# Turns of pairs 16 to 18 issued together, with the loads of two batches held behind them

## Chip, cores and metric

One Trainium2 chip, one core. The metric is device time in microseconds of one execution, lower is better; runs are compared by their median.

## The reference

Attention with 16 extra "beacon" keys ahead of the 576 causal ones, for 8 batches of 8 heads of 64, and behind it a mixer with a low-rank token mix and a two-layer MLP over the 512 channels:

```
scores = (q @ concat(beacon_k, k).T) / sqrt(64), causal over the last 576 keys
attn   = softmax(scores) @ concat(beacon_v, v)
x      = attn as (8, 576, 512)
u      = x + (x.T @ U @ V).T
out    = u + relu(u @ w_ch1) @ w_ch2          # 512 -> 2048 -> 512
```

## The kernel before

The work is in f16, with f32 in PSUM. A pair is two heads of one batch; there are 32 pairs, four to a batch, so pairs 16 to 19 are batch 4 and pairs 20 to 23 batch 5. The tokens of all batches are cut into blocks of 512 for the MLP, whose work is cut into small units (four matmuls each) that wait in a list.

The order of everything is written out by hand: a string `SCRIPT` of short words, which `step` turns into instructions one after the other. Each engine works through its own instructions in that order and waits where an operand isn't there. A plain number n takes n MLP units from the list. The other words that matter here:

- `k5`, `q5`, `b5`, `v4`: loads of that batch's k, q, beacon k and v, issued on POOL (GpSimd) with a cast from f32 to f16 (`k_loads`, `q_loads`, L184 and L190; `v_loads`, L187 and L197). k and q go to the tiles `hd` (the first tokens) and `st` (the other 512); there are two of each, so batch n + 2 takes the place of batch n.
- `GkA16`: regroup, the copy of pair 16's k from `st` into the pair's tile `pr` (three of them). The letter before the number names the engine: A for ScalarE (ACT, L518), V for VectorE (DVE, L247), G for POOL.
- `R16`: the turn of pair 16, a DMA transpose of `pr` into a tile `raw` (three of them), issued on SP (L277). A batch's first turned pair issues ahead of it two more DMA transposes that turn the first tokens of all its heads (L270, `qT<-hd`, `kT<-hd`).
- `TkV16`, `TqA16`: the copy of the turned k or q from `raw` into the order of tokens, on the engine of the letter (DVE L285, ACT L518).
- `Sa16`, `Sb16`: the pair's scores (PE, L311) and their exponentials (ACT, L317). `M16`: the causal mask (DVE, L298 and L300). `A16.0`: exp times v for one head (PE, L335), then its sums' reciprocal and the product (DVE, L343 and L344).
- `X3.0` to `X3.2`: the low-rank mix of a batch; `x12`: a DMA transpose of attention output (SP, L355).
- MLP units: first layer (PE, L435), ReLU on ACT (L439) or DVE (L441); second layer (PE, L452), the sum with `ut` on DVE (L465), the store on SP (L470). The first unit of a block also issues four DMA transposes of `uT` into `ut` on SP (L425).
- `Z16`: a copy of one element of pair 16's `raw` into a scratch element, on POOL. `step` has the word; the string before doesn't use it.

Eight PSUM banks are shared by all of PE's outputs, so PE stops when ACT and DVE don't empty them. The kernel's guard (a check of the softmax sums at the end, with a general path that isn't taken) plays no part here.

Of the kernel before, what the change touches and what calls it, by code (L numbers as in the profile page):

```python
# [27 lines left out]
def kernel(  # L28
# [605 lines left out]
    def step(t):  # L634
# [58 lines left out]
        TqV8 2 GkV10 1 A6.0 GqA10 TqA10 q3 1 A7.1 A7.0 2 X1.0 X1.1 X1.2 TkA10 TqV9 TkV9 1 TkA8 1 Sa9 Sa8 3 Sb8  # L693
        1 k3 GqA11 1 v3 Sb9 M8 2 A8.1 A8.0 1 GkV12 1 GqV12 Sa10 1 M9 GkV11 R12 Sb10 1 M10 1 TkV11 1 A10.0
        TqA11 4 GkA13 A9.1 A9.0 Sa11 1 TkV12 GqV15 Sb11 1 k4 A10.1 2 GkA14 GqV13 1 TqA12 b5 Sa12 1 GqA14 M11
        R13 R14 3 GkA15 Sb12 1 A11.0 1 TkV13 M12 A11.1 q4 b4 TqA13 Sa13 R15 A12.0 TkA14 TqV14 1 TqV15 1 GkA16
        GqA16 1 R16 2 Sb13 v4 1 A12.1 M13 X2.0 2 Sb14 GkA17 A13.0 X2.1 TkV15 X2.2 A13.1 Sa14 GqA17 R17 Sb15 k5
        q5 GqA18 1 M14 1 Sa15 x12 3 TkV16 A14.1 TqA16 1 A14.0 k6 4 M15 GkA18 x13 1 R18 TkA17 1 TqV17 Sb16 2
        Sa16 A15.1 GkA19 M16 2 A15.0 TqA18 2 GqA19 x14 GkV20 x15 1 GkA21 1 R19 Sa17 1 A16.0 Sb17 2 GqV20 A16.1
        1 M17 TkA18 Sb18 X3.0 2 X3.1 1 Sa18 A17.0 1 GqA21 M18 1 X3.2 1 TkA19 R20 1 R21 1 GkV22 b6 1 TqA19  # L700
        A18.0 A18.1 v5 1 A17.1 Sa19 4 x18 1 Sb19 TqV20 TkV20 2 M19 GqA22 1 x16 R22 Sb20 A19.1 q6 Sa20 3 M20 1
        TkA21 x17 1 A19.0 1 TqA21 1 A20.0 TqV22 v6 1 GkV23 GqA23 1 x19 R23 Sa21 TkV22 X4.0 1 k7 1 Sb21 1 M21 1
        X4.1 1 A20.1 Sa22 1 A21.0 1 GkV25 GqV24 1 TqA23 GkV24 1 b7 R24 1 TkV23 Sb22 1 q7 A21.1 x20 X4.2 1
        GqA26 M22 GqV25 4 Sa23 x21 A22.0 TkA24 1 Sb23 R25 1 M23 2 A22.1 1 TqA24 A23.1 GkA26 1 R26 Sa24 2 A23.0
        2 Sb24 x22 2 TkA25 TqA25 v7 5 GqV27 1 M24 GkV27 Sa25 2 x23 TkV26 1 A24.0 R27 1 Sb25 TqV26 M25 X5.0
        A24.1 GqV28 2 Sb26 1 GkA28 R28 A25.0 2 x24 Sa26 TqV27 1 X5.1 4 X5.2 1 GkV30 1 TkA27 M26 1 TkV28 A25.1
        GkV29 Sa27 GqV29 2 Sb27 1 A26.0 x25 1 R29 1 M27 A26.1 TqV28 GqA30 1 R30 A27.1 GkV31 2 Sa28 A27.0 1 x26
        1 TqV29 Sb28 2 M28 2 GqV31 TqA30 1 TkA29 TkA30 Sa29 1 X6.0 R31 Sb29 A28.1 x27 A28.0 4 TkV31 2 TqV31 1
        M29 1 Sa30 1 A29.0 2 x28 X6.1 2 Sb30 A29.1 X6.2 4 x29 Sa31 M30 10 Sb31 A30.0 A30.1 2 x30 M31 4 A31.0
        A31.1 2 X7.0 4 x31 1 X7.1 3 X7.2 2  # L710
    """

    with tc.manual_schedule(engines={ENG.PE, ENG.Activation, ENG.DVE, ENG.SP, ENG.Pool}):
# [118 lines left out]
```

## Time and profile before

| | |
|---|---|
| median of 3 runs | 359.29 us (359.05 to 359.36) |
| the profiled execution's own time | 361.73 us |
| its span, first to last instruction | 360.1 us |
| granted TensorE clock, mean | 0.993 |
| PE busy | 347.2 us, 96% |
| ACT, DVE, POOL busy | 205.2, 189.9, 84.0 us |
| DMA queue of POOL's loads | 17.54 MB written, 51.8% of 16 engines' span |
| DMA queue of SP's transfers | 25.14 MB, 34.9% |

PE is the matmuls, PEld the weight loads that run beside them; SPq and POOLq are the sequencers that issue DMAs. An idle time in square brackets is that of the engine just before the instruction, with what ended it. All starts are in us from the span's start.

### The profile page before, as it was taken

The numbers are of one execution on the slowest core, as the hardware profiler recorded it, in microseconds if no ns is written. First come the engines' busy times: TensorE is split into PE (matmuls) and PEld (weight loads), VectorE is DVE, ScalarE is ACT, GpSimd is POOL, SyncE is SP. The second block draws the span as 40 slices with busy tenths as digits, with TensorE's granted clock in tenths as the row PEclk, the third lists the DMA queues.
The fourth block names the chain that finished last, engine by engine and source line by source line (L and its number), as shares of the span: only waits on it lengthen the run. The fifth ranks groups of instructions, "written<-read, shape, count | busy, mean of one in ns | idle before, by whom it ended". The sixth has DMA issues, their size and how long they took to land.

```text
span 360.1 us, 7694 instructions
## 1 busy us (share of the span) xinstructions
PE 347.2 (96%) x3022; PEld 177.2 (49%) x3022; DVE 189.9 (53%) x530; ACT 205.2 (57%) x432; POOL 84.0 (23%) x123
## 2 busy tenths in 40 slices
PE   7789999999999989999999999999999999999995
PEld 3455478844545435454444444454544544444444
DVE  3775355546649454574767427675554447313311
ACT  4885867399579868658653963678335302401300
POOL 7966648601308005400630050000000000000000
PEclk9989999999999999999999999999999999999998
DMA  9999999992959999996899694563333123013112
GB/s 191 174 172 187 183 191 164 202 160 40 164 127 129 117 162 111 175 223 106 94 163 194 139 107 107 111 116 61 88 100 66 20 76 103 16 58 90 31 48 76
DMA packets 134396, 43.57 MB, mean 121 GB/s; under 512 B 106545, under 2 KB 130353, under 8 KB 134353
## 3 DMA queue, kind: packets, MB, share of 16 engines
q0 software_dynamic: 69008, 17.54, 51.8%
q1 hardware_dynamic: 64752, 25.14, 34.9%
q8 instruction: 25, 0.41, 0.5%
q10 hardware_dynamic: 592, 0.34, 0.3%
q14 instruction: 19, 0.15, 0.1%
HBM read 37.63 MB, written 9.44 MB: 131 GB/s over the span
## 4 chain that ended last, share of the span: by engine, by line
PE 86%; DMA 6%; DVE 2%; ACT 2%; SPq 1%; issue 1%
PE cps L452 35%; PE gps L435 32%; PE po L335 8%; PE sps L311 7%; DMA raw<-pr 4%; DMA sth<-in_q_dram 2%; ACT expt L317 1%; DMA stm<-in_q_dram 1%; PE tps L257 1%; PE ups L394 1%; PE ups L401 1%; PE qtp L375 1%; SPq L190 1%; DVE xb L344 1%; SPq L184 1%
## 5 line engine op out<-in xcount | busy, mean ns | idle before, releaser
L317 ACT ACTIVATE expt<-sps 128x496 f16<-128x496 f32 (+2 forms) x256 | 111.6, 544 | 43.2 <-PE sps L311 39.2
L452 PE MATMUL cps<-w,gT 128*128 128x512 f16 (+1 forms) x656 | 134.2, 353 | 0.0
L435 PE MATMUL gps<-uT,w 128*128 128x512 f16 x576 | 132.7, 379 | 1.1 <-DVE xb L344 1.1
L439 ACT ACTIVATE gT<-gps 128x512 f16<-128x512 f32 x86 | 52.2, 625 | 70.4 <-PE gps L435 70.2
L452 PEld LDWEIGHTS <-gT 128*128 128x128 f16 x656 | 60.5, 98 | 57.5 <-issue 4.4
L435 PEld LDWEIGHTS <-w 128*128 128x128 f16 x576 | 53.0, 98 | 65.1 <-issue 3.5
L441 DVE TENSOR_SCALAR gT<-gps 128x512 f16<-128x512 f32 x58 | 40.0, 690 | 49.5 <-PE gps L435 48.6
L465 DVE TENSOR_TENSOR ob<-cps,ut 128x512 f32<-128x512 f32 (+1 forms) x33 | 22.2, 674 | 47.0 <-PE cps L452 46.6
L335 PEld LDWEIGHTS <-expt 128*128 128x128 f16 (+1 forms) x960 | 36.0, 99 | 14.5 <-DVE expt L298 4.0
L197 POOL DMA_DIRECT2D vs<-in_v_dram x50 | 40.0, 811 | 7.2 <-DMA st<-in_k_dram 4.0
L335 PE MATMUL po<-vs,expt 128*128 128x65 f16 (+1 forms) x960 | 39.2, 195 | 2.3 <-ACT expt L317 1.4
L311 PE MATMUL sps<-qT,kT 64*128 64x80 f16 (+4 forms) x384 | 35.7, 282 | 2.1 <-ACT expt L317 1.2
L344 DVE TENSOR_TENSOR xb<-po,rec 128x320 f16<-128x320 f32 x64 | 31.5, 492 | 2.2
L298 DVE TENSOR_TENSOR expt<-expt,bigmask 128x512 f16<-128x512 f16 x64 | 26.7, 418 | 9.2 <-ACT expt L317 9.2
L343 DVE RECIPROCAL rec<-po 128x5 f32<-128x5 f32 x64 | 12.0, 188 | 28.0 <-PE po L335 27.2
L311 PEld LDWEIGHTS <-kT 64*128 64x128 f16 x384 | 12.5, 94 | 24.4 <-issue 16.4
L187 POOL DMA_DIRECT2D vs<-in_beacon_v_dram x10 | 5.4, 540 | 68.1 <-PE po L335 68.0
L408 DVE TENSOR_TENSOR uT<-ups,xt 128x240 f16<-128x240 f32 (+3 forms) x40 | 15.6, 450 | 7.2 <-PE ups L401 7.2
L518 ACT ACTIVATE pr<-st 128x512 f16<-128x512 f16 x26 | 16.8, 658 | 0.8 <-DMA st<-in_k_dram 0.8
L190 POOL DMA_DIRECT2D st<-in_k_dram x8 | 6.8, 856 | 40.7 <-ACT gT L439 22.9
L518 ACT ACTIVATE qT<-raw 128x512 f16<-128x512 f16 x10 | 11.1, 1105 | 5.3 <-DMA raw<-pr 5.3
L300 DVE TENSOR_TENSOR expt<-expt,mask 80x80 f16<-80x80 f16 x64 | 12.2, 191 | 0.0
(78 smaller groups left out, 170.7 us busy)
## 6 DMA issues: line engine op xcount, KB each, us to landing
out_dram<-ob SPq DMA_DIRECT2D x31, 256.0 KB, 2.2
st<-in_q_dram POOLq DMA_DIRECT2D x6, 512.0 KB, 9.8
st<-in_k_dram POOLq DMA_DIRECT2D x6, 512.0 KB, 8.4
vs<-in_v_dram POOLq DMA_DIRECT2D x18, 128.0 KB, 6.7
w<-in_moe_w_ch_dram POOLq DMA_DIRECT2D x4, 512.0 KB, 8.8
w<-in_moe_w_ch_dram POOLq DMA_DIRECT2D x2, 1024.0 KB, 12.1
out_dram<-ob SPq DMA_DIRECT2D x10, 128.0 KB, 5.7
stm<-in_k_dram SPq DMA_DIRECT2D x4, 256.0 KB, 4.6
```

Source lines behind the costliest of these rows:

```text
L197: nc.gpsimd.dma_start(out=dst[a : a + nq[j], j, :, :], in_=src[hs, ds(q0[j], nq[j]), :].rearrange("h p d -> p h d"))
L298: nc.vector.tensor_tensor(out=e4, in0=e4, in1=bigmask, op=ALU.min)
L311: nc.tensor.matmul(ps[g, i][:, ds(o, w)], kT[hp, c, ds(P * ch, P)], qT[hp, c, ds(qa, w)], start=True, stop=True,)
L317: nc.scalar.activation(out=ex[i][:, ds(PAD + SLOT * g, gw[g])], in_=ps[g, i][:, 0 : gw[g]], func=AF.Exp, scale=scale)
L335: nc.tensor.matmul(po[:, j, :], ex[0 : nk[c], ds(blk[(c, j)], P)], vs[0 : nk[c], ds(c * H * E + h * E, E)], start=(c == 0), stop=(c == j),)
L344: nc.vector.tensor_tensor(out=xb[:, h // 2, :, ds(D * (h % 2), D)], in0=po[:, :, 0:D], in1=r.broadcast_to([P, NT, D]), op=ALU.mult)
L435: nc.tensor.matmul(g[:, 0:n], w1[:, cc, ts(dc, P)], uT[:, cc, ds(ring(t0), n)], start=(cc == 0), stop=(cc == NCC - 1))
L439: nc.scalar.activation(out=gT["t"][:, dc, 0:n], in_=g[:, 0:n], func=AF.Relu)
L441: nc.vector.tensor_scalar_max(out=gT["t"][:, dc, 0:n], in0=g[:, 0:n], scalar1=0.0)
L452: nc.tensor.matmul(ps[:m, :], gT["t"][:, dc, ds(P * i, m)], w2[:, dc, ds(cs, w)], start=(dc == 0), stop=turned and dc == NDC - 1, skip_gro ...
L465: nc.vector.tensor_tensor(out=ob[:m, :], in0=ps[:m, :], in1=gT["u"][:m, i, ds(cs, w)], op=ALU.add)
L518: nc.scalar.activation(out=out, in_=in_, func=AF.Copy)
```

## The change

Only the string changes. Pair 16's two regroups move from ACT to DVE and, with its turn R16, to the place right behind R15. Z16 is put ahead of the loads of v4. Pair 18's k regroup moves from ACT to DVE; both its regroups and its turn R18 move to the place right behind R17. Z18 is put ahead of the loads k5 and q5. As POOL works in order, a Z holds all loads behind it until that turn has landed. The MLP units between the words are as many as before.

```diff
-        R13 R14 3 GkA15 Sb12 1 A11.0 1 TkV13 M12 A11.1 q4 b4 TqA13 Sa13 R15 A12.0 TkA14 TqV14 1 TqV15 1 GkA16
-        GqA16 1 R16 2 Sb13 v4 1 A12.1 M13 X2.0 2 Sb14 GkA17 A13.0 X2.1 TkV15 X2.2 A13.1 Sa14 GqA17 R17 Sb15 k5
-        q5 GqA18 1 M14 1 Sa15 x12 3 TkV16 A14.1 TqA16 1 A14.0 k6 4 M15 GkA18 x13 1 R18 TkA17 1 TqV17 Sb16 2
+        R13 R14 3 GkA15 Sb12 1 A11.0 1 TkV13 M12 A11.1 q4 b4 TqA13 Sa13 R15 GkV16 GqV16 R16 A12.0 TkA14 TqV14
+        1 TqV15 4 Sb13 Z16 v4 1 A12.1 M13 X2.0 2 Sb14 GkA17 A13.0 X2.1 TkV15 X2.2 A13.1 Sa14 GqA17 R17 GqA18
+        GkV18 R18 Sb15 Z18 k5 q5 1 M14 1 Sa15 x12 3 TkV16 A14.1 TqA16 1 A14.0 k6 4 M15 x13 1 TkA17 1 TqV17
...
```

More of the change, by code (lines that the diff above doesn't have):

```diff
@@ L695 @@
         TqA11 4 GkA13 A9.1 A9.0 Sa11 1 TkV12 GqV15 Sb11 1 k4 A10.1 2 GkA14 GqV13 1 TqA12 b5 Sa12 1 GqA14 M11
-        R13 R14 3 GkA15 Sb12 1 A11.0 1 TkV13 M12 A11.1 q4 b4 TqA13 Sa13 R15 A12.0 TkA14 TqV14 1 TqV15 1 GkA16
-        GqA16 1 R16 2 Sb13 v4 1 A12.1 M13 X2.0 2 Sb14 GkA17 A13.0 X2.1 TkV15 X2.2 A13.1 Sa14 GqA17 R17 Sb15 k5
-        q5 GqA18 1 M14 1 Sa15 x12 3 TkV16 A14.1 TqA16 1 A14.0 k6 4 M15 GkA18 x13 1 R18 TkA17 1 TqV17 Sb16 2
-        Sa16 A15.1 GkA19 M16 2 A15.0 TqA18 2 GqA19 x14 GkV20 x15 1 GkA21 1 R19 Sa17 1 A16.0 Sb17 2 GqV20 A16.1
@@ L700 @@
[L700 to L709, printed above, removed]
@@ L710 @@
-        A31.1 2 X7.0 4 x31 1 X7.1 3 X7.2 2
+        R13 R14 3 GkA15 Sb12 1 A11.0 1 TkV13 M12 A11.1 q4 b4 TqA13 Sa13 R15 GkV16 GqV16 R16 A12.0 TkA14 TqV14
+        1 TqV15 4 Sb13 Z16 v4 1 A12.1 M13 X2.0 2 Sb14 GkA17 A13.0 X2.1 TkV15 X2.2 A13.1 Sa14 GqA17 R17 GqA18
+        GkV18 R18 Sb15 Z18 k5 q5 1 M14 1 Sa15 x12 3 TkV16 A14.1 TqA16 1 A14.0 k6 4 M15 x13 1 TkA17 1 TqV17
+        Sb16 2 Sa16 A15.1 GkA19 M16 2 A15.0 TqA18 2 GqA19 x14 GkV20 x15 1 GkA21 1 R19 Sa17 1 A16.0 Sb17 2
+        GqV20 A16.1 1 M17 TkA18 Sb18 X3.0 2 X3.1 1 Sa18 A17.0 1 GqA21 M18 1 X3.2 1 TkA19 R20 1 R21 1 GkV22 b6
@@ new lines @@
+        1 TqA19 A18.0 A18.1 v5 1 A17.1 Sa19 4 x18 1 Sb19 TqV20 TkV20 2 M19 GqA22 1 x16 R22 Sb20 A19.1 q6 Sa20
+        3 M20 1 TkA21 x17 1 A19.0 1 TqA21 1 A20.0 TqV22 v6 1 GkV23 GqA23 1 x19 R23 Sa21 TkV22 X4.0 1 k7 1 Sb21
+        1 M21 1 X4.1 1 A20.1 Sa22 1 A21.0 1 GkV25 GqV24 1 TqA23 GkV24 1 b7 R24 1 TkV23 Sb22 1 q7 A21.1 x20
+        X4.2 1 GqA26 M22 GqV25 4 Sa23 x21 A22.0 TkA24 1 Sb23 R25 1 M23 2 A22.1 1 TqA24 A23.1 GkA26 1 R26 Sa24
+        2 A23.0 2 Sb24 x22 2 TkA25 TqA25 v7 5 GqV27 1 M24 GkV27 Sa25 2 x23 TkV26 1 A24.0 R27 1 Sb25 TqV26 M25
@@ L711 @@
+        X5.0 A24.1 GqV28 2 Sb26 1 GkA28 R28 A25.0 2 x24 Sa26 TqV27 1 X5.1 4 X5.2 1 GkV30 1 TkA27 M26 1 TkV28
+        A25.1 GkV29 Sa27 GqV29 2 Sb27 1 A26.0 x25 1 R29 1 M27 A26.1 TqV28 GqA30 1 R30 A27.1 GkV31 2 Sa28 A27.0
+        1 x26 1 TqV29 Sb28 2 M28 2 GqV31 TqA30 1 TkA29 TkA30 Sa29 1 X6.0 R31 Sb29 A28.1 x27 A28.0 4 TkV31 2
+        TqV31 1 M29 1 Sa30 1 A29.0 2 x28 X6.1 2 Sb30 A29.1 X6.2 4 x29 Sa31 M30 10 Sb31 A30.0 A30.1 2 x30 M31 4
+        A31.0 A31.1 2 X7.0 4 x31 1 X7.1 3 X7.2 2
     """
```

## The prediction

> **What bounds the kernel now.** I read the page first. Its columns in the engine lines are busy us, share of the span, number of instructions; the two last lines belong to the chain that ended last.
>
> ```profile
> span 360.1 us, 7694 instructions
> PE 347.2 (96%) x3022; PEld 177.2 (49%) x3022; DVE 189.9 (53%) x530; ACT 205.2 (57%) x432; POOL 84.0 (23%) x123
> PE 86%; DMA 6%; DVE 2%; ACT 2%; SPq 1%; issue 1%
> PE cps L452 35%; PE gps L435 32%; PE po L335 8%; PE sps L311 7%; DMA raw<-pr 4%; DMA sth<-in_q_dram 2%; ACT expt L317 1%; DMA stm<-in_q_dram 1%; PE tps L257 1%; PE ups L394 1%; PE ups L401 1%; PE qtp L375 1%; SPq L190 1%; DVE xb L344 1%; SPq L184 1%
> ```
>
> TensorE (PE) is the bound; a change of order can only win back PE's idle time. The 6% of DMA looks like a big prize, but the chain follows whoever was last, and while it stands on a DMA the PE may still be multiplying. So the second view is the chain in order of time around the turn in question (start, us, what):
>
> ```profile
> 116.10 13.06 DMA raw<-pr
> ```
>
> That DMA is R16, pair 16's turn: issued at 116.10, landed at 129.16. The third view asks what PE lost meanwhile: busy time in consecutive stretches (stretch, its length, then PE, PEld, DVE, ACT, POOL with instruction counts, granted clock, DMA share, GB/s).
>
> ```profile
> 95.00:108.00 13.00, 13.00 (x115) 6.06 (x112) 6.53 (x19) 10.19 (x21) 0.00 (x0) 1.00 0.82 150
> 108.00:124.00 16.00, 15.33 (x203) 8.65 (x200) 12.39 (x35) 15.34 (x37) 7.86 (x10) 1.00 1.47 130
> 124.00:130.00 6.00, 5.49 (x39) 2.51 (x37) 0.92 (x3) 1.38 (x3) 0.00 (x0) 1.00 1.50 138
> 130.00:136.00 6.00, 5.07 (x38) 2.05 (x39) 4.40 (x11) 6.00 (x13) 0.00 (x0) 1.00 1.15 156
> 136.00:150.00 14.00, 14.00 (x144) 6.88 (x140) 7.38 (x22) 11.19 (x23) 8.40 (x11) 1.00 1.24 136
> ```
>
> PE idles 16.00 - 15.33 = 0.67, 6.00 - 5.49 = 0.51 and 6.00 - 5.07 = 0.93 us, together **2.11 us**, and nothing in the stretches on either side. That is the ceiling for this change: 0.6% of the span, not 4%. The granted clock is 1.00 throughout, so no clock is to be won. The timelines of PE, ACT and DVE (start, length, instruction, idle before it and what ended it) say which idle it is:
>
> ```profile
> 113.32 0.48 PE L311 MATMUL sps<-qT,kT 64*128 64x208 f16 x2 [0.30 <-ACT expt L317]
> 114.03 0.62 PE L335 MATMUL po<-vs,expt 128*128 128x65 f16 x15 [0.23 <-ACT expt L317]
> 130.56 1.04 PE L435 MATMUL gps<-uT,w 128*128 128x512 f16 x4 [1.07 <-DVE xb L344]
> 129.18 1.18 ACT L518 ACTIVATE qT<-raw 128x512 f16<-128x512 f16 x1 [4.62 <-DMA raw<-pr]
> 129.19 0.70 DVE L285 COPY kT<-raw 128x512 f16<-128x512 f16 x1 [5.06 <-DMA raw<-pr]
> ```
>
> DVE and ACT both stop in order at pair 16's reorder copies (TkV16, TqA16) for 5.06 and 4.62 us. PE had multiplications ready for 5.06 - 1.07 = 4.0 us of it, then stood 1.07 us because nobody emptied its PSUM banks. The 0.51 + 0.93 = 1.44 us around 130 are this stop and the queue on ACT behind it (ACT is busy for 6.00 of 6.00 us there). The 0.30 + 0.23 at 113 to 114 are ACT being late with exponentials.
>
> **The change, part by part.** SP and POOL around it, from their timelines and, for R17, from the rows of line L277 (ns min/median/max of the issue, first and last start); then five landing rows of source lines, for, in this order, the three turns before R16, for R16 and R17, for R18, for v4's five main loads, and for the main loads of k5 (min) and q5 (max):
>
> ```profile
> 106.44 1.30 SPq L277 DMA_TRANSPOSE raw<-pr  x1
> 112.62 0.34 SPq L470 DMA_DIRECT2D out_dram<-ob  x1
> 113.05 1.21 SPq L270 DMA_TRANSPOSE qT<-hd  x1
> L277 SPq DMA_TRANSPOSE raw<-pr x1: 4588/4588/4588, 119.8 to 119.8; - x1
> 124.47 7.97 SPq L425 DMA_TRANSPOSE ut<-uT  x4
> 108.58 0.52 POOL L187 DMA_DIRECT2D vs<-in_beacon_v_dram  x1 [15.44 <-PE po L335]
> 109.09 4.19 POOL L197 DMA_DIRECT2D vs<-in_v_dram  x5
> 113.25 0.91 POOL L190 DMA_DIRECT2D st<-in_k_dram  x1
> 114.80 0.92 POOL L190 DMA_DIRECT2D st<-in_q_dram  x1
> DMA to landing us min/median/max: 3.1/3.1/3.2
> DMA to landing us min/median/max: 12.2/12.6/13.1
> DMA to landing us min/median/max: 4.5/4.5/4.5
> DMA to landing us min/median/max: 3.6/4.6/5.8
> DMA to landing us min/median/max: 10.8/13.2/15.6
> ```
>
> A turn alone takes 3.1 us; with v4, k5 and q5 in flight it takes 12.2 to 13.1.
>
> 1. *R16 earlier.* It now stands right behind R15, ahead of the output store at 112.62. SP is free from 106.44 + 1.30 = 107.74. The two head turns issue at about 107.8 and 109.0 (1.21 us for the first, the second taken alike). The pair's regroup copies sit on DVE behind head 11.1 and ahead of head 12.0, that is at 109.8 (row below), so the raw turn can issue at about 110.4 and, alone in the DMA engines, lands at 110.4 + 3.1 = 113.5, say **114**. Its readers come at 124.1 (129.19 - 5.06): 10 us early, so the 5.06 and 4.62 us of waiting are gone, and with them up to 1.44 us of PE idle. R16's three issues end near 111.7, before the store's data are there (112.62), so nothing behind it on SP is delayed.
>
> 2. *Regroups from ACT to DVE.* Three copies, q16, k16 and k18:
>
> ```profile
> 111.63 1.17 ACT L518 ACTIVATE pr<-st 128x512 f16<-128x512 f16 x2
> 97.90 0.29 DVE L247 COPY pr<-st 128x512 f16<-128x512 f16 x1
> 109.79 0.18 DVE L343 RECIPROCAL rec<-po 128x5 f32<-128x5 f32 x1
> 113.53 0.43 DVE L298 TENSOR_TENSOR expt<-expt,bigmask 128x512 f16<-128x512 f16 x1 [0.31 <-ACT expt L317]
> ```
>
> ACT loses 1.17 us just ahead of the exponentials that PE waited for by 0.30 + 0.23 = 0.53 us, so that idle should go too. DVE gains 2 x 0.29 = 0.58 us at 110 and 0.29 us at 118; it stands idle for ACT by 0.31 at 113.53, which hides half of the first, so 0.58 - 0.31 = 0.27 is left at worst. The second falls into the 16.00 - 12.39 = 3.6 us that DVE is idle between 108 and 124. I charge 0 to 0.27 us and take 0.1, since PE waited for ACT there, not for DVE.
>
> 3. *Z16, v4 held.* A one-element copy on POOL, not in this trace; its price lies between nothing and the 0.52 us that POOL's small beacon load takes, and POOL has nothing else to do there. v4 moves from 108.58 to about 114 (5.5 us later); it lands by 114 + 4.7 (its six issues) + 5.8 = 124.5. Its first reader, head 16.0, stands in the string behind GkV20, which ran at 139.78 (row under 5). Free.
>
> 4. *R17, R18, then Z18.* R17 was issued at 119.8, when ACT's q17 copy was done; q18's copy now follows on ACT at once, so R18 issues one issue later (1.30 us), near 121, ahead of the four ut turns (124.47). These are needed by the first output sum at 141.88 (row under 5): over 10 us of cover for a delay of 1.3 to 4.6 us, the shortest and the longest issue of a turn. With only v4's tail in flight I put R18's landing between the quiet 3.1 and the crowded 13.1 us, nearer to 4.5 (R18 before, with four ut and two xt turns about it): 125 to 127.
>
> 5. *k5 and q5 held.* POOL stops at Z18, with k5, q5 and then k6 behind it. k5 issues at about 126 in place of 113.25.
>
> ```profile
> 139.78 0.48 DVE L247 COPY pr<-st 128x512 f16<-128x512 f16 x1
> 140.72 1.13 ACT L518 ACTIVATE pr<-st 128x512 f16<-128x512 f16 x2
> 141.88 0.69 DVE L465 TENSOR_TENSOR ob<-cps,ut 128x512 f32<-128x512 f32 x1 [1.61 <-PE cps L452]
> 144.46 0.28 DVE L247 COPY pr<-st 128x512 f16<-128x512 f16 x1
> ```
>
> k5 took 10.8 us to land, so it was there at 124.1 and first read at 139.78 (GkV20): 15.7 us early. The hold spends 12.8 of that. With the same 10.8 us it lands at 137, the reader having moved up to 137.8. q5, issued 114.80 - 113.25 = 1.6 us behind k5, lands by 127.6 + 15.6 = 143 at worst; its first reader (GqV20) comes at 144.46 - 2 = 142.5. Both are narrow, and a late one costs PE nothing until the 4.0 us of cover measured above are used up. k6 waits for ACT's last reading of batch 4's k, GkA19, which the hold doesn't move.
>
> The Trainium skill, page DMA: Bandwidth & Descriptors, section Rules for kernel authors, speaks against this part: issue a DMA early and wait on its semaphore late. By it each us of hold would be a loss; here the 15.7 us between k5's landing and its first reader show that there was time to give away, and the trace only warns that the hold takes nearly all of it.
>
> **Sum.** 1.44 (the stop at 130 and its queue) + 0.53 (exponentials at 113) - 0.1 (DVE copies) = 1.87 us; a little less, 1.8, because PE's ends are modelled. The profiled execution took 361.73 us with a span of 360.1; I expect a span of 358.3. Its time lies 2.4 us over the median of the three runs (359.29); the difference is carried over as it is: 359.29 - 1.8 = **357.5 us**. Does it reach the end? The stretch from 140 on, and the chain's last piece:
>
> ```profile
> 140.00:361.00 221.00, 215.69 (x1642) 102.23 (x1640) 109.36 (x274) 102.98 (x201) 21.05 (x28) 0.99 0.60 98
> 342.20 13.87 PE cps L452 x80
> ```
>
> Of 221.00 - 215.69 = 5.3 us, 0.9 lie beyond the span and 360.1 - 356.1 = 4.0 behind PE's last matmul. PE is as good as never idle in between, and each later load is released by the engines' own progress, so the chain moves up as a whole.
>
> **Rivals.** (a) *The wait passes on to pair 17*, whose k copy on ACT is this row:
>
> ```profile
> 132.68 1.20 ACT L518 ACTIVATE kT<-raw 128x512 f16<-128x512 f16 x1
> ```
>
> Without the stop ACT reaches it near 132.68 - 4.62 = 128.1. If R17 takes 13.1 us beside v4, as R16 did, it lands at 132.9: a stop of 4.8 us, of which 4.0 are covered; 0.8 and the queue behind it on ACT (1.44 - 1.07 = 0.4) stay, 357.5 + 1.2 = 358.7. For: R17's 12.2 us before. Against: k5 and q5, two thirds of that traffic, are no longer there.
>
> (b) *The held loads come late: slower.* R18 lands late, POOL releases k5 late, DVE stands at GkV20 and ACT at GkA21 (140.72), ahead of pair 17's exponentials. With R18 at 121 + 13.1 = 134.1, k5 lands at 134.3 + 10.8 = 145.1, against a reader at 137.8: 7.3 us, less 4.0 of cover, costs 3.3 us: 357.5 + 3.3 = 360.8. It outweighs the gain when k5 lands after 137.8 + 4.0 + 1.8 = 143.6, that is R18 after 132.6, 11.6 us from its issue. For: R16 and R17 did take 12.2 and 13.1. Against: those had v4, k5 and q5 around them, R18 has the tail of v4 alone. This is the outcome to which the Trainium skill's rule quoted above (DMA: Bandwidth & Descriptors, Rules for kernel authors) points.
>
> (c) *No difference that can be measured.* The idle is that of one profiled execution, which took 361.73 - 359.29 = 2.4 us more than the median; if R16 landed earlier in the others, the stop wasn't there to be removed: 359.3. Against: the span, 360.1, is itself close to the median, and a landing 9 us behind the quiet one is no matter of a few per cent.
>
> **How the numbers follow.** Forecast 0.66, (a) 0.15, (b) 0.15, (c) 0.04. About 0.2% (0.7 us) is what a measurement of this kernel tells from no change: faster means under 358.6, slower over 360.0. The forecast's own range is 356.8 (all 2.11 and some more in the modelled ends) to 358.3 (only the 1.07 us that PE shows at 130). (a) gives half of its chance to faster, half to same; (c) is same. So faster 0.66 + 0.07 = 0.73, same 0.08 + 0.04 = 0.12, slower 0.15. The range 356.8 to 359.4 holds the forecast, (a) and (c), and leaves (b) out.
>
> **What would show it.** Right: R16's raw turn issued near 110 and landed near 114; no wait of ACT or DVE for raw between 120 and 140; PE idle between 108 and 136 under 0.5 us; v4 issued near 114, k5 near 126, and GkV20 without a wait for st. Wrong: a wait of TkA17 or TqV17 for raw (a); k5 landing after 141 with DVE or ACT idle "<-DMA st" (b); PE idle between 136 and 150, which showed 14.00 of 14.00 before; or a shorter PE idle with no shorter median (c).

## The result, and the profile after

The changed kernel takes **357.51 us** (median of 8 runs, 356.67 to 358.17) against 359.49 us before (8 runs, 358.56 to 360.78): a ratio of 0.9943, 95% interval 0.9925 to 0.9960, 2.0 us saved. The prediction's base, 359.29 us, was the median of the first 3 of the 8 runs before. The profiled execution took 357.74 us, span 356.0.

The page after, its head and its chain:

```profile
span 356.0 us, 7697 instructions
PE 344.6 (97%) x3022; PEld 175.6 (49%) x3022; DVE 189.4 (53%) x533; ACT 203.9 (57%) x429; POOL 84.7 (24%) x125
PE 79%; DVE 2%; ACT 1%; issue 0%
```

Two instructions more on POOL (Z16 and Z18), three moved from ACT to DVE, and no DMA in this chain, which the profile follows back from the end to 58.6 us. The stretches of the prediction, in the kernel after (same columns):

```profile
108.00:124.00 16.00, 15.20 (x194) 8.35 (x190) 12.54 (x37) 15.72 (x35) 5.13 (x7) 1.00 1.05 102
124.00:130.00 6.00, 6.00 (x36) 2.63 (x34) 3.12 (x8) 3.96 (x8) 3.54 (x5) 1.00 0.95 143
130.00:136.00 6.00, 6.00 (x56) 2.98 (x55) 3.93 (x11) 5.78 (x13) 1.29 (x2) 1.00 1.56 146
136.00:150.00 14.00, 14.00 (x142) 6.41 (x139) 7.14 (x21) 9.07 (x20) 6.64 (x10) 1.00 1.56 173
```

PE's idle of 0.51 and 0.93 us around 130 is gone. In the first stretch 0.80 us is idle, no less than before (0.67); with it the prediction's sign of under 0.5 us between 108 and 136 was missed. PE now waits for other engines there, as its timeline says.

```profile
112.10 0.63 PE L335 MATMUL po<-vs,expt 128*128 128x65 f16 x15 [0.49 <-DVE expt L298]
118.76 0.35 PE L311 MATMUL sps<-qT,kT 64*128 64x464 f16 x1 [0.17 <-ACT expt L317]
122.46 0.61 DVE L285 COPY kT<-raw 128x512 f16<-128x512 f16 x1
122.24 1.22 ACT L518 ACTIVATE qT<-raw 128x512 f16<-128x512 f16 x1
```

The two last rows, from DVE's and ACT's timelines, are pair 16's reorder copies: no idle time in brackets where 5.06 and 4.62 us stood. The turns and loads behind that, from SP's and POOL's timelines, then the landing rows of R16, of R17 and R18 together, and of the main loads of k5 (min) and q5 (max), and DVE's first reading of k5 and of q5:

```profile
106.37 1.20 SPq L270 DMA_TRANSPOSE qT<-hd  x1
109.04 1.95 SPq L277 DMA_TRANSPOSE raw<-pr  x1
117.75 3.73 SPq L277 DMA_TRANSPOSE raw<-pr  x2
112.98 0.18 POOL L665 COPY gate<-raw 1x1 f16<-1x1 f16 x1 [21.30 <-DMA raw<-pr]
113.50 0.53 POOL L187 DMA_DIRECT2D vs<-in_beacon_v_dram  x1 [0.34 <-PE ups L401]
L190 POOL DMA_DIRECT2D st<-in_k_dram x1: 885/885/885, 126.1 to 126.1; - x1
DMA to landing us min/median/max: 3.9/3.9/3.9
DMA to landing us min/median/max: 6.4/6.7/7.1
DMA to landing us min/median/max: 7.9/10.6/13.3
135.21 0.48 DVE L247 COPY pr<-st 128x512 f16<-128x512 f16 x1
141.03 0.29 DVE L247 COPY pr<-st 128x512 f16<-128x512 f16 x1 [0.60 <-DMA st<-in_q_dram]
```

R16 issues at 109.0 and lands at 112.9, 9 us ahead of its readers. k5 is issued at 126.1 and lands at 134.0, 1.2 us ahead of its reader; q5 lands at 141.0, 0.60 us too late.

The two spans differ by 4.1 us, twice the medians' difference. To compare two single executions, take the same two instructions in both, here the 16 second-layer matmuls ahead of the changed words and those behind them (PE timelines: before, then after):

```profile
101.62 3.63 PE L452 MATMUL cps<-w,gT 128*128 128x512 f16 x16
138.23 3.62 PE L452 MATMUL cps<-w,gT 128*128 128x512 f16 x16
...
100.16 3.63 PE L452 MATMUL cps<-w,gT 128*128 128x512 f16 x16
134.12 3.62 PE L452 MATMUL cps<-w,gT 128*128 128x512 f16 x16
```

That is 36.61 us before and 33.96 after: between these two executions the stretch that holds the changed words shrank by **2.65 us** (e3 below shows that single executions can differ by 1 us of it), and PE stays 4.1 us ahead from there to the end. The other 101.62 - 100.16 = 1.46 us were there before the first changed word. They belong to the start: in the first 30 us the granted clock was 0.94 in the one execution and 1.00 in the other, and PE had begun 288 matmuls against 309 (before, then after).

```profile
0.00:30.00 30.00, 23.64 (x288) 13.21 (x289) 19.41 (x84) 20.33 (x48) 23.37 (x45) 0.94 1.26 181
0.00:30.00 30.00, 24.30 (x309) 13.60 (x310) 20.97 (x89) 22.10 (x54) 23.08 (x44) 1.00 1.25 182
```

### The profile page after: what moved, and what is told of

It is laid out like the page before. It is cut to its first block, busy times and chain, and to the rows that moved or that the text cites. A ratio compares the mean times of both kernels' runs of the same rounds, so it can differ in the third digit from the quotient of the medians.

```text
span 356.0 us, 7697 instructions
## 1 busy us (share of the span) xinstructions
PE 344.6 (97%) x3022; PEld 175.6 (49%) x3022; DVE 189.4 (53%) x533; ACT 203.9 (57%) x429; POOL 84.7 (24%) x125
## 4 chain that ended last, share of the span: by engine, by line
PE 79%; DVE 2%; ACT 1%; issue 0%
PE cps L452 33%; PE gps L435 31%; PE po L335 7%; PE sps L311 6%; PE ups L401 1%; PE ups L394 1%; PE qtp L375 1%; ACT expt L317 1%; PE tps L257 1%; DVE xb L344 0%; DVE qT L285 0%; ACT qT L518 0%; ACT pr L518 0%; DVE ob L465 0%; DVE expt L298 0%
## 5 line engine op out<-in xcount | busy, mean ns | idle before, releaser
L452 PE MATMUL cps<-w,gT 128*128 128x512 f16 (+1 forms) x656 | 134.2, 353 | 0.0
L335 PEld LDWEIGHTS <-expt 128*128 128x128 f16 (+1 forms) x960 | 35.1, 98 | 14.0 <-DVE expt L298 3.4
L335 PE MATMUL po<-vs,expt 128*128 128x65 f16 (+1 forms) x960 | 38.4, 194 | 2.1 <-DVE expt L298 1.9
L311 PE MATMUL sps<-qT,kT 64*128 64x80 f16 (+4 forms) x384 | 34.9, 282 | 2.0 <-ACT expt L317 1.1
L311 PEld LDWEIGHTS <-kT 64*128 64x128 f16 x384 | 12.2, 94 | 23.4 <-issue 15.8
L518 ACT ACTIVATE pr<-st 128x512 f16<-128x512 f16 x23 | 14.8, 663 | 1.6 <-DMA st<-in_k_dram 1.5
L247 DVE COPY pr<-st 128x512 f16<-128x512 f16 x32 | 9.7, 321 | 4.6 <-DMA st<-in_q_dram 3.9
L300 DVE TENSOR_TENSOR expt<-expt,mask 80x80 f16<-80x80 f16 x64 | 12.2, 190 | 0.0
```

Of the source, the lines that this page charges most:

```text
L311: nc.tensor.matmul(ps[g, i][:, ds(o, w)], kT[hp, c, ds(P * ch, P)], qT[hp, c, ds(qa, w)], start=True, stop=True,)
L335: nc.tensor.matmul(po[:, j, :], ex[0 : nk[c], ds(blk[(c, j)], P)], vs[0 : nk[c], ds(c * H * E + h * E, E)], start=(c == 0), stop=(c == j),)
L452: nc.tensor.matmul(ps[:m, :], gT["t"][:, dc, ds(P * i, m)], w2[:, dc, ds(cs, w)], start=(dc == 0), stop=turned and dc == NDC - 1, skip_gro ...
```

## The experiments

The change has three parts: an earlier turn, copies on another engine, held loads. Theory T: the turns' late landing under the loads is what costs. Rivals: the copies taken off ACT carry the gain (A), or the holds do (H). Each run was measured by its median, with the ratio to the kernel before on the same chip (its medians were 359.73 us beside e1 to e4, 359.54 beside e5 to e8 and 360.38 beside e9 and e10, so the ratios are to be compared), and by the stretch between the two instructions above, in one profiled execution each; a longer stretch ends at the second-layer matmuls that start at 150.14 before.

| run | short stretch | long stretch | median | ratio, 95% interval |
|---|---|---|---|---|
| before | 36.61 | 48.52 | 359.49 | |
| changed | 33.96 | 45.87 | 357.51 | 0.9943 (0.9925 to 0.9960) |
| e1 R16 early, no holds | 33.68 | 45.59 | 357.54 | 0.9933 (0.9908 to 0.9958) |
| e2 holds only | 34.08 | 52.32 | 364.02 | 1.0121 (1.0092 to 1.0151) |
| e3 copies on DVE only | 35.59 | 47.50 | 359.59 | 0.9990 (0.9968 to 1.0013) |
| e4 changed, no holds | 34.19 | 46.10 | 357.75 | 0.9944 (0.9922 to 0.9966) |
| e5 holds, R18 early, R16 late | 34.58 | 46.48 | 358.24 | 0.9975 (0.9948 to 1.0001) |
| e6 hold 4 us longer | 33.95 | 46.38 | 357.88 | 0.9949 (0.9928 to 0.9970) |
| e7 hold 8 us longer | 33.92 | 51.06 | 363.48 | 1.0109 (1.0071 to 1.0146) |
| e8 as e1, copies on ACT | 34.11 | 46.01 | 357.68 | 0.9940 (0.9918 to 0.9962) |
| e9 e1, q15 later | 34.24 | 46.15 | 357.66 | 0.9931 (0.9905 to 0.9956) |
| e10 e1, k16 on ACT | 33.56 | 45.47 | 357.13 | 0.9921 (0.9894 to 0.9948) |

**e1: the early turn alone.**

```diff
-        ... Sa13 R15 A12.0 TkA14 TqV14 1 TqV15 1 GkA16 GqA16 1 R16 2 Sb13 v4 1
+        ... Sa13 R15 GkV16 GqV16 R16 A12.0 TkA14 TqV14 1 TqV15 4 Sb13 v4 1
```

> Only the first part: pair 16's regroups on DVE and its turn R16 right behind R15; no holds, pair 18 as before. The measure is the time from the 16 matmuls of the second layer that start at 101.62 in the kernel before to those at 138.23: 36.6 us there, 34.0 in the changed kernel. Theory T (R16's late landing under loads is what costs): R16 issues at 109, only 1.5 us after v4's first load, and lands before its readers at 123; R17 stays under v4, k5 and q5, lands near 132 and stops ACT at TkA17 (rival a). So 34.5 to 35.5, median 0.3 to 0.5% faster. Theory H (the holds carry the gain): 36.6. Theory A (ACT's relief by the moved regroups carries it): 34.0 to 34.5.

33.68 us, below every range that was expected, and the median as far down as with the whole change. The turn shares the DMA engines with v4, which starts before it (the two second-layer groups of PE, SP's and POOL's timelines, the landing rows of R16 and of R17, then ACT's copy of R17's k):

```profile
100.44 3.63 PE L452 MATMUL cps<-w,gT 128*128 128x512 f16 x16
134.12 3.62 PE L452 MATMUL cps<-w,gT 128*128 128x512 f16 x16
109.33 1.88 SPq L277 DMA_TRANSPOSE raw<-pr  x1
107.40 0.52 POOL L187 DMA_DIRECT2D vs<-in_beacon_v_dram  x1 [15.45 <-PE po L335]
DMA to landing us min/median/max: 7.0/7.0/7.0
DMA to landing us min/median/max: 9.1/9.1/9.1
128.09 1.20 ACT L518 ACTIVATE kT<-raw 128x512 f16<-128x512 f16 x1
```

R16 takes 7.0 us instead of 13.06 and lands at 116.3; R17, issued at 118.25, lands at 127.4, 0.7 us before ACT's copy of it (128.1). So rival (a) came close, but cost nothing; ACT waits 0.37 us for R18 at 134.90, and PE doesn't. H falls: no hold is needed for the gain. A isn't settled by this run, since it moves the copies too.

**e2: the holds alone.**

```diff
-        ... 1 R16 2 Sb13 v4 1 ... R17 Sb15 k5 q5 GqA18
+        ... 1 R16 2 Sb13 Z16 v4 1 ... R17 Sb15 Z17 k5 q5 GqA18
```

> Only holds: Z16 ahead of v4 and Z17 ahead of k5 and q5, every turn and regroup where it was before. T: R16, issued at 113 to 116, is alone in the DMA engines and lands near 120, before its readers at 124, so the stop goes though R16 isn't issued earlier; ACT's 0.5 us at 113 stays: 34.3 to 35.0, median 0.4 to 0.6% faster. If the earlier issue is what counts: 36.6. Theory A: 36.6, since ACT has all its copies.

Half right. R16 at its old place, with the loads held, lands in 3.1 us and pair 16's stop is gone: the short stretch is 34.08. But the stop comes back two pairs later. R18, which T had not looked at, is now issued behind k5 and q5 (SP's timeline, its landing row, ACT's and PE's timelines, and the stretches behind with the clock in the third column from the end):

```profile
128.22 4.74 SPq L277 DMA_TRANSPOSE raw<-pr  x1
DMA to landing us min/median/max: 12.6/12.6/12.6
140.81 1.06 ACT L518 ACTIVATE qT<-raw 128x512 f16<-128x512 f16 x1 [6.94 <-DMA raw<-pr]
143.43 0.25 PE L311 MATMUL sps<-qT,kT 64*128 64x208 f16 x1 [4.07 <-ACT expt L317]
140.00:144.00 4.00, 0.37 (x2) 0.09 (x1) 0.00 (x0) 3.19 (x6) 1.75 (x2) 1.00 1.38 182
144.00:148.00 4.00, 4.00 (x25) 1.94 (x25) 0.00 (x0) 3.11 (x7) 1.31 (x2) 0.57 1.80 194
```

ACT stands 6.94 us, PE 4.07, and afterwards the clock is at half for 4.00 x (1 - 0.57) / 0.5 = 3.4 us. This is what the second half of the change is for: once k5 and q5 are held, R18 has to go ahead of them.

**e3: the copies on DVE alone.**

```diff
-        ... 1 TqV15 1 GkA16 GqA16 1 R16 ... 4 M15 GkA18 x13
+        ... 1 TqV15 1 GkV16 GqV16 1 R16 ... 4 M15 GkV18 x13
```

> Only the engine of three regroups (k16, q16, k18) changes from ACT to DVE, at their old places. T: the stop at 130 stays, at most the 0.53 us of PE's waiting for ACT at 113 goes: 36.0 to 36.6, median the same within 0.2%. Theory A: 34.0 to 34.8, median 0.5% faster.

The median doesn't move, as T says. DVE still stops at pair 16, and PE's wait ahead of it has only changed its engine, from 0.30 + 0.23 us for ACT to 0.91 us for DVE (DVE's and PE's timelines):

```profile
127.87 0.70 DVE L285 COPY kT<-raw 128x512 f16<-128x512 f16 x1 [4.55 <-DMA raw<-pr]
113.21 0.63 PE L335 MATMUL po<-vs,expt 128*128 128x65 f16 x15 [0.91 <-DVE expt L298]
129.25 1.04 PE L435 MATMUL gps<-uT,w 128*128 128x512 f16 x4 [0.56 <-DVE xb L344]
```

The stretch of this one execution is 1.0 us shorter than before, outside what T expected: its stop was 4.55 us instead of 5.06, PE's idle behind it 0.56 us instead of 1.07, and the four score matmuls next to that took 1.06 us instead of 1.57. The length of the stop differs between executions; a single profile of it is worth no better than that 1 us.

**e4: the whole change without Z16 and Z18.**

```diff
-        ... Sb13 Z16 v4 ... GkV18 R18 Sb15 Z18 k5 q5 1
+        ... Sb13 v4 ... GkV18 R18 Sb15 k5 q5 1
```

> The changed kernel without Z16 and Z18: turns as in it, loads as early as in the kernel before. T: as e1, R16 early enough; R17 and R18 under all loads, landing 8 to 13 us after their issue, a stop of up to 4 us at TkA17 that is mostly covered: 34.3 to 35.5. H: 36.6. If the holds are worth nothing: 34.0.

34.19 and 357.75 us: within the runs' scatter the same as with the holds. R16 lands 6.3 us after its issue, R17 8.2 and R18 7.7, all in time, and the stop of up to 4 us at TkA17 that I expected isn't there.

**e5: the holds with R18 in front of them, R16 late.**

```diff
-        ... 1 R16 2 Sb13 v4 1 ... R17 Sb15 k5 q5 GqA18 1 M14 ... GkA18 x13 1 R18 TkA17
+        ... 1 R16 2 Sb13 Z16 v4 1 ... R17 GqA18 GkV18 R18 Sb15 Z18 k5 q5 1 M14 ... x13 1 TkA17
```

> The changed kernel's second half with R16 left late: regroups of pair 16 on ACT and R16 at their old place, Z16 ahead of v4; R18 behind R17 and Z18 ahead of k5 and q5 as in the changed kernel. From the matmuls at 101.62 to those at 150.14 the kernel before takes 48.5 us, the changed one 45.9. If the 4.1 us of PE idle in the kernel with holds only came from R18 issued behind the held loads, it goes with R18 in front of them: 46.0 to 46.8 here and the median 0.3 to 0.6% faster. If holding v4 and k5 as such is what costs, 49 to 52.

46.48 us against e2's 52.32: with R18 ahead of the held loads e2's stop is gone, so the cause named there is shown. The median is 0.36% below the kernel before on the same chip (359.54). The ratio, 0.9975 with an interval that reaches to 1.0001, leaves a gain over the kernel before unproven; one of the twelve executions took 362.69 us, the next longest 359.07.

**e6 and e7: the hold made longer**, by fills of a scratch tile on POOL, 11 and 22 of them.

```diff
-        GkV18 R18 Sb15 Z18 k5 q5 1
+        GkV18 R18 Sb15 Z18 D11 k5 q5 1        # e7: D22
```

> The changed kernel with k5 and q5 held some 4 us longer: 11 fills of a scratch tile on POOL behind Z18. k5 then lands near 138 against a reader at 135.2 (it landed at 134.0), q5 near 145 against 140.4. The prediction's cover of 4.0 us: stops of 3 and 4.6 us on DVE and ACT, PE loses 0 to 0.8 us; 45.9 to 46.8 from the matmuls at 101.62 to those at 150.14 of the kernel before. Without cover (each us late is a us lost): 49 or more.

> The same with 22 fills, some 8 us. k5 near 142, 6.8 us late. With a cover of 4.0 us PE loses about 3 us for k5, and up to 1 more for q5 (near 149): 48.5 to 50, which is about the kernel before, the point that the prediction's rival b puts at k5 landing 4.0 us and the gain after its reader. Without cover: 52 or more.

k5 is issued at 129.3 in e6 and 134.2 in e7 (126.1 in the changed kernel, whose stretch starts 0.7 us later than that of e6 and 0.4 us later than that of e7). DVE's first reading of it and PE's longest wait, e6 first, then e7 with the two stretches around and behind it:

```profile
138.00 0.30 DVE L247 COPY pr<-st 128x512 f16<-128x512 f16 x1 [3.40 <-DMA st<-in_k_dram]
139.66 0.25 PE L311 MATMUL sps<-qT,kT 64*128 64x208 f16 x1 [0.20 <-ACT expt L317]
...
141.32 0.29 DVE L247 COPY pr<-st 128x512 f16<-128x512 f16 x1 [6.47 <-DMA st<-in_k_dram]
142.27 0.51 PE L311 MATMUL sps<-qT,kT 64*128 64x336 f16 x6 [2.80 <-DVE ob L465]
140.00:144.00 4.00, 1.53 (x11) 0.66 (x11) 1.49 (x4) 2.62 (x6) 1.72 (x2) 0.95 1.60 183
144.00:148.00 4.00, 4.00 (x27) 1.96 (x27) 0.98 (x3) 2.22 (x5) 1.75 (x2) 0.62 1.42 221
```

A stop of 3.40 us on DVE costs PE 0.20 us of idle, one of 6.47 us costs 2.80: the cover is 3.40 - 0.20 = 3.2 to 6.47 - 2.80 = 3.7 us, against 4.0 in the prediction. e6 came out as expected, e7 did not: its long stretch is 51.06 - 45.87 = 5.2 us over the changed kernel, where 3 to 4 were expected. PE's idle explains 2.80 + 0.20 of it (0.20 is a second wait at 142.98); the lower clock in the two stretches explains, by estimate, another 4.00 x (1 - 0.95) + 4.00 x (1 - 0.62) = 1.7. The other 0.5 us stay unexplained; e6 is as much longer than the changed kernel, 46.38 - 45.87, with only 0.20 us of idle.

**e8: e1 with the copies left on ACT.**

```diff
-        ... Sa13 R15 A12.0 TkA14 TqV14 1 TqV15 1 GkA16 GqA16 1 R16 2 Sb13 v4 1
+        ... Sa13 R15 GkA16 GqA16 R16 A12.0 TkA14 TqV14 1 TqV15 4 Sb13 v4 1
```

> As e1 (R16 early, no holds), but pair 16's two regroups stay on ACT and move with the turn. T: R16 issues near 110 and lands near 117, still 5 us before its readers, so the stop is gone; ACT has its 1.2 us of copies ahead of the exponentials as before: 34.1 to 34.8 from the matmuls at 101.62 to those at 138.23, median 0.4 to 0.6% faster. If the move to DVE is needed for it: 35.5 to 36.6.

34.11 us (PE's two groups start at 99.84 and 133.95) and 0.9940: the engine of the copies makes no difference that can be measured, the turn's place does. With e3 this settles rival A.

**e9 and e10: e1, with less on DVE in front of pair 13's mask**, the 0.50 us that e1 has left.

```diff
-        ... TkA14 TqV14 1 TqV15 4 Sb13 v4 ... X2.1 TkV15 X2.2      # e9
+        ... TkA14 TqV14 5 Sb13 v4 ... X2.1 TqV15 TkV15 X2.2
-        ... R15 GkV16 GqV16 R16                                    # e10
+        ... R15 GkA16 GqV16 R16
```

> e1 (R16 early, regroups on DVE, no holds) and pair 15's reorder copy of q (TqV15) moved from its place ahead of pair 13's masks to the place ahead of TkV15. In e1 PE's only idle left between 98 and 180 is 0.50 us at 111.9, waiting for pair 13's mask on DVE, which the two regroups have made late. With 0.6 us of copy taken from in front of that mask the idle should go: 33.1 to 33.4 us from the matmuls at 101.62 to those at 138.23 of the kernel before, against 33.7 in e1; the median 0.7% under the kernel before. If the mask waits for something else: 33.7.

> e1 with only q16's regroup on DVE and k16's on ACT, both at the early place. DVE has 0.25 us less ahead of the mask, ACT 0.65 more ahead of the exponentials: 33.3 to 34.0 over the same stretch; if ACT's copy is what PE waits for next, 34.0 or more.

e9 missed with 34.24 us: the wait for the mask shrinks from 0.50 to 0.34 us, and the copy, moved to a busier place, makes PE wait there (PE's timeline):

```profile
111.49 0.63 PE L335 MATMUL po<-vs,expt 128*128 128x65 f16 x15 [0.34 <-DVE expt L298]
115.08 1.09 PE L311 MATMUL sps<-qT,kT 64*128 64x336 f16 x8 [0.27 <-DVE kT L285]
116.53 1.90 PE L435 MATMUL gps<-uT,w 128*128 128x512 f16 x8 [0.36 <-DVE xb L344]
```

e10 has the shortest stretch (33.56, inside the range expected) and the lowest ratio (0.9921), but its interval overlaps those of e1 and of the changed kernel, so it isn't shown to be better than they are.

## Why the prediction was right

Forecast 357.5 us, measured 357.51. The mechanism was right, R16's late landing and the stops of DVE and ACT behind it, and the size nearly so: 1.8 us of saving were forecast and 2.0 measured. The exact hit is luck: the base was 359.49 us over 8 runs and not 359.29, two terms were mis-sized in opposite directions, and the ceiling of 2.11 us didn't hold for the two profiled executions, which differ by 2.65. The span forecast beside it, 358.3 us, was 2.3 too long; 1.46 of that is the start.

1. *R16 earlier* was the right mechanism, and by e1 and e8 it is the whole of the gain. In e2 the short stretch has no stop either, though R16 keeps its old place; so the landing is what counts. Issue and landing came as worked out: 109.0 and 112.9, where 110.4 and 114 were written. The execution after is 1.46 us ahead from its start; with this added they are 110.5 and 114.4, and the starts below move alike.
2. *Its size*, 1.44 us, was too small for these two executions. It was read from PE's idle time; by the starts of the same matmuls, the part of the stretch behind the head's product (L335) that starts at 124.56 before and 122.97 after shrank from 13.67 us to 11.15 in the changed kernel, 2.5 us. PE's ends are modelled, and matmuls that come one by one count as mostly busy, as the same four score matmuls show (PE's timelines, before and after):

```profile
133.89 1.57 PE L311 MATMUL sps<-qT,kT 64*128 64x496 f16 x4
130.94 0.58 PE L311 MATMUL sps<-qT,kT 64*128 64x496 f16 x4
```

   1.57 us in place of 0.58, shown without an idle time. That they wait for PSUM banks, which ACT is late to empty, is likely but not shown: the trace names nothing that releases them. I named the modelled ends, but subtracted for them where they had to be added. The medians moved by only 2.0 us, and e3's stop was 0.5 us shorter than this one's; so part of the 2.5 us may belong to the profiled execution.
3. *ACT's 0.53 us* was too large. In the changed kernel the part ahead of that product gained 22.94 - 22.81 = 0.13 us, in e1 0.41. The two copies on DVE make pair 13's mask late, so the wait changed its engine: 0.49 us for DVE in place of 0.30 + 0.23 for ACT. The 0.1 us charged for the copies was too little, and so was their upper bound, 0.27. The changed kernel adds 0.17 us of waiting for ACT at 118.76, where q18's copy now stands ahead of the exponentials; the sum had no term for it.
4. *v4 held, R17 and R18.* v4 was issued at 113.5 (114 written) and nobody waited for it. R18 landed at 125.5, inside the 125 to 127 that I took, but 6.4 us after its issue, where I leaned to 4.5. R17 took 7.1 us, and its readers found it there. Rival (a) priced R17 by R16 and R17 before, as if both had stood beside v4: v4's last load was issued at 112.5 and took at most 5.8 us, so it had landed before R17's issue at 119.8.
5. *k5 and q5 held.* k5 was issued at 126.1 as written and landed at 134.0 (137 written); q5 landed at 141.0 and 0.60 us late (143 and 0.5 us late written), with no idle of PE. That the reader comes so close behind was right; what the hold is worth I never priced, and by e1 and e4 it brings nothing that can be measured.
6. *Rival (b)* didn't happen, and e7 made it happen: the 4.0 us of cover measured 3.2 to 3.7, and its price per late us was right for the idle but left out the clock. The rule of the Trainium skill weighed there (DMA: Bandwidth & Descriptors, Rules for kernel authors: issue early, wait late) is borne out by e1 against the changed kernel: with R16 issued earlier, loads left early cost nothing. In the kernel before the same early loads made R16 late. e2 and e7 show what a hold can cost, 4.3 and 3.9 us.
7. *Rival (a)* came within 0.7 us in e1; *rival (c)* is refuted by the interval of the ratio, which ends at 0.9960.

## What to carry to other kernels

Here a transfer on the path was made safe by issuing it earlier, without any hold; holding back the traffic around it moved the wait to the transfer queued behind the hold, until that went in front too. Measure a stop by the start times of the same instructions in two profiles, not by the idle time alone, and do so behind the start-up: the first of the two matmul groups started anywhere from 99.28 to 101.62 us in these twelve profiles, which is more than the change is worth. An engine's in-order stop was free here up to the work that the bound engine had ready, 3.2 to 4.0 us, and dear after that.

## What the runs showed that I had not expected

An idle of PE of 2.80 us (e7) or 4.07 us (e2), each with another 0.20 us close behind it, is followed by about 3.4 us at half clock: in stretches of half a microsecond the granted clock reads 0.50 from 144.5 to 147.5 in e2 and from 144.0 to 147.0 in e7. The idle of 1.07 us in the kernel before left the clock at 1.00. So a stop that outran its cover by 3 to 4 us cost some 1.7 us more than its idle time, an estimate from 3.4 us at half clock. The Trainium skill (TensorE: Matmul & The Clock Gate, Why this matters for your kernels) asks for no idle gaps over about 3 us; here 2.80 was enough.

A turn lands 3.1 us after its issue when it is alone. Behind loads, the number of them doesn't give the delay: with v4, k5 and q5 issued early, R17 took 12.2 us in the kernel before, 9.1 in e1 and 8.2 in e4. What the traces show is that the first turn issued behind the loads lands together with the last of them. In the kernel before, R17 lands at 132.0 and q5's last load (its first tokens, into `hd`) at 132.2; in e1 they land at 127.4 and 127.6; in e2, R18 lands at 140.8 and that load at 141.1. The two are some 0.3 us apart at most in all eight profiles that have this order (before, e1 to e4, e8 to e10), and beside v4 alone, in the changed kernel, R17 lands at 124.9 and v4's last load at 124.8. R16 before, issued while POOL was still issuing q5's last load, landed 3 us ahead of it. Why a turn waits for the loads ahead of it isn't shown, but it fits what e1 and e2 found: it helps a turn not to be issued behind them.
